# Moving batch 0's k and v tails from GpSimd's DMA queue to SyncE's, in halves of the heads

## Chip, cores and metric

The kernel runs on one core of one Trainium2 chip. The metric is the device time of one execution in microseconds, as the median of several runs; smaller is better. Times inside a run are counted from the first instruction of the profiled execution.

## The reference

Eight batches of eight heads, 576 positions, head dimension 64. Queries and keys pass a ReLU and are multiplied by a cosine and by a sine of the position, which doubles their width to 128; attention is linear (no softmax); a feed-forward layer with a leaky ReLU follows.

```python
theta = np.pi / 2.0 * pos / S                     # S = 576
phi(x) = concat([relu(x) * cos, relu(x) * sin])   # 64 -> 128
kv  = einsum('bhsf,bhsd->bhfd', phi(k), v)
z   = sum(phi(k), axis=2)
num = einsum('bhsf,bhfd->bhsd', phi(q), kv)
den = einsum('bhsf,bhf->bhs', phi(q), z) + 1e-6
x   = (num / den) -> (B*S, H*D) = (4608, 512)
out = leaky_relu(x @ w_in) @ w_out                # 512 -> 2048 -> 512, slope 0.01
```

## The kernel before

**Tiles.** The 576 positions of a batch are split into a main part of 512 (four positions on each of 128 partitions, `J = 4`) and a tail of 64. The main part of q, k or v of one batch is a tile of 128 partitions by 8 heads by 4 by 64; `load_main` (line 88) fetches it in halves of four heads for batch 0, in pieces of 1024 bytes. The tails of k and v are packed with two heads on the 128 partitions, even heads on even partitions and odd heads on odd ones: `load_kvtail` (line 98) makes one tile of 128 by 4 head pairs by 64 and fills it with two DMAs, one for each parity `o`, of 64 KB each in pieces of 256 bytes.

**Batch 0.** Its arrival starts the kernel and nothing can be computed ahead of it. SyncE issues, in this order (lines 147 to 155): q heads 0-3 and 4-7, k heads 0-3 (called k0 below), v heads 0-3 (v0), k heads 4-7 (k1), v heads 4-7 (v1), and then the eight pieces of the first weight matrix, `w1st`. GpSimd issues the four tail DMAs on its own queue (lines 210, 211) after it has made the constants.

**Compute of batch 0** (lines 554 to 608), written out by hand in the order in which each engine runs it:
- q is rotated (line 241 on VectorE, 239 on ScalarE), transposed on TensorE (line 366) and copied out of PSUM.
- `k_tail` rotates all four head pairs of k's tail with two VectorE instructions into `kpt`; `k_main(0, j, ...)` rotates heads 0-3 of the main part into `kpm`, five instructions on VectorE and three on ScalarE.
- `v_tail` multiplies v's tail by a parity mask, once for each parity (`vtail`: ScalarE line 222, VectorE line 224); `v_main` casts v's main part to fp16 into `vmain` (VectorE line 249, ScalarE line 247).
- `kv_half(0, 0, "t", 14)` runs 28 matmuls on a blank tile (line 168; they only keep TensorE busy), then the k-by-v products of heads 0-3: 16 matmuls over the main part (line 290) and two over the tail (line 299). ScalarE copies the sum out as `kv` (line 323).
- The same follows for heads 4-7: `k_main(0, j, ..., 4, 8)`, and `v_main` for these heads on GpSimd (line 249); `num_half(0, jp, 0)` forms numerator and denominator of heads 0-3 (line 417) and divides on VectorE (`den` line 392, `rden` line 396, `xp` line 397); then `kv_half(0, 1, "t", 2)`, transposes of the quotients (line 434), `num_half(0, jp, 1)` for heads 4-7, and the first feed-forward matmuls (line 460).

TensorE runs its program in the order in which it is written, so that `kv_half(0, 1)`, the transposes of `xp` and the two `num_half(0, jp, 1)` wait for one another in that order. After batch 0 the matmuls of the feed-forward layer follow without a break; batches 1 to 7 load their tails on SyncE's queue already.

**Queues.** A DMA on SyncE's queue signals one of eight semaphores, taken in turn. A DMA therefore is not issued before the one eight places ahead of it on that queue has landed. GpSimd's queue has semaphores of its own.

Of the kernel before, what the change touches and what calls it, by code (L numbers as in the profile page):

```python
# [9 lines left out]
dt = mybir.dt  # L10
# [3 lines left out]
P = 128  # L14
J = 4
# [3 lines left out]
def kernel(  # L19
# [14 lines left out]
    nc = tc.nc  # L34
    B, H, S, D = q.shape
# [43 lines left out]
    st = {}  # L79
# [8 lines left out]
    def load_main(nm, src, b, parts=(0, 1), soon=False):  # L88

        if parts[0] == 0:  # L90
            st[nm, b] = staged([P, H, J, D], f"{nm}st", soon)
        lo, hi = 4 * parts[0], 4 * parts[-1] + 4
        nc.sync.dma_start(  # L93
            st[nm, b][:, lo:hi],
            src[b, lo:hi, 0:MAIN, :].rearrange("h (p j) d -> p h j d", j=J),
        )

    def load_kvtail(nm, src, b, eng=nc.sync):

        t = kvtail.tile([P, H // 2, D], dt.float32, name=f"{nm}tl", tag="kvtail")  # L100
        v4 = src[b, :, MAIN:S, :].rearrange("(c o) p d -> o p c d", o=2)
        for o in range(2):
            eng.dma_start(t[o:P:2], v4[o])
        st[nm + "t", b] = t

    def load_qtail(i):
        if i == 0:
# [112 lines left out]
    def masked(eng, o, i, col):  # L220
        if eng is ACT:
            nc.scalar.activation(o, i, AF.Copy, scale=col)
        else:
            eng.tensor_scalar(out=o, in0=i, scalar1=col, scalar2=None, op0=ALU.mult)
# [37 lines left out]
        k_part(b, j, 0, eng_c, lo, hi)  # L262
        k_part(b, j, 1, eng_s, lo, hi)

    def k_tail(b, eng_c, eng_s):
        k_part(b, J, 0, eng_c)
        k_part(b, J, 1, eng_s)

    def k_part(b, j, part, eng, lo=0, hi=H):
        c = j if j < J else J + 1  # L270
        col, f = (cos_t, sin_t)[part][:, c : c + 1], part * D
        if j < J:
            o, i = st["kpm", b][:, lo:hi, j, f : f + D], st["k", b][:, lo:hi, j, :]
        else:
            o, i = st["kpt", b][:, :, f : f + D], st["kt", b]
# [5 lines left out]
    def v_tail(b, eng, both=(0, 1)):  # L281
        for o in both:
            masked(eng, vtail[:, :, o, 0:D], st["vt", b], odd[:, o : o + 1])

    def kv_mm(b, hg, ps):
        kpm, kpt = st["kpm", b], st["kpt", b]
# [31 lines left out]
    def kv_half(b, hg, where, blanks=0):  # L318
        ps = psum(where, [P, MAIN], dt.float32, "ps_kvh")
        idle(blanks, ps)  # L320
        ps = ps[:, 0 : 4 * NE]
        kv_mm(b, hg, ps)
        nc.scalar.copy(
            kv[b][:, 4 * hg : 4 * hg + 4, 0 : NE - 1],
            ps.rearrange("p (h e) -> p h e", h=4)[:, :, 0 : NE - 1],
        )
# [235 lines left out]
            idle(1, ps_idle)  # L562
    for j, eng in ((0, ACT), (1, DVE), (2, DVE), (3, ACT)):
        q_copy(0, j, eng)
    k_tail(0, DVE, DVE)
    for j, c, s in ((0, DVE, DVE), (3, ACT, ACT), (1, DVE, DVE), (2, DVE, ACT)):
        k_main(0, j, c, s, 0, 4)
    v_tail(0, ACT, (0,))
    v_tail(0, DVE, (1,))
    v_main(0, 0, 2, DVE)  # L570
    v_main(0, 2, 4, ACT)
    kv_half(0, 0, "t", 14)
    for j, c, s in ((0, DVE, DVE), (3, ACT, ACT), (1, DVE, DVE), (2, DVE, ACT)):
        k_main(0, j, c, s, 4, 8)
    v_main(0, 4, 6, POOL)
    v_main(0, 6, 8, POOL)
    num_half(0, 0, 0, "s", 2)
# [826 lines left out]
```

## Time and profile before

| | us |
|---|---|
| three runs | 270.31, 270.94, 272.93 |
| median | 270.94 |
| the profiled execution's own time | 271.15 |
| its span, first to last instruction | 269.2 |
| around the span (difference of the two) | 1.95 |

The page of the profile gives the busy time of each engine over the span, a strip of 40 slices, the DMA queues, the chain of work that ended last, and the costliest groups of instructions. TensorE (PE) is granted its full clock in every slice. Other views of the same trace are the timeline (start, duration, engine, source line, operation, output and input, count, and in square brackets how long the engine had been idle and what released it), the chain in order of time, the view of one tile or line (with "DMA to landing", the time from a DMA's issue to the arrival of its last byte), the waits, and the table by windows (busy us of each engine with its number of instructions, then TensorE's clock, the mean busy share of the 16 DMA engines, and the GB/s that they moved).

### The profile page before, as it was taken

The page shows a single profiled execution, that of the slowest core. Times are in us where ns is not written, and L with a number is a line of the kernel's source. Part 1 is how long each engine was busy: PE and PEld are TensorE (multiplying, and loading weights), DVE is VectorE, ACT ScalarE, POOL GpSimd, SP SyncE. Part 2 cuts the span into 40 slices and gives each one's busy share as a digit, 9 for nine tenths or more (in the row PEclk, how much of TensorE's full clock was granted, in tenths as well). Part 3 has the DMA queues.
Part 4 walks back from the last instruction along what each step waited for, and adds up shares of the span by engine and source line. Part 5 has one row for each costly group of instructions (what it writes and reads, how often), then busy time and mean ns, then how long its engine had stood idle before and what let it go on. Part 6 is the DMA issues. An engine that isn't in the chain of part 4 may idle for free.

```text
span 269.2 us, 6819 instructions
## 1 busy us (share of the span) xinstructions
PE 263.1 (98%) x2742; PEld 230.1 (85%) x2742; DVE 215.8 (80%) x486; ACT 203.9 (76%) x347; POOL 13.1 (5%) x25
## 2 busy tenths in 40 slices
PE   8989999999999999999999999999999999999994
PEld 6976465666899989999999999999999999999983
DVE  5785798698997898897979797979789968966453
ACT  8756556695989998997798799888968757787621
POOL 5057001000000000000000000000000000000000
PEclk9999999999999999999999999999999999999999
DMA  6999999979999969999999799987267232200314
GB/s 221 380 394 413 394 367 376 366 140 285 285 248 285 193 206 245 360 168 256 270 238 140 247 280 185 173 243 162 65 102 178 45 74 67 111 2 0 156 41 117
DMA packets 86190, 57.05 MB, mean 212 GB/s; under 512 B 55632, under 2 KB 81232, under 8 KB 85648
## 3 DMA queue, kind: packets, MB, share of 16 engines
q1 hardware_dynamic: 85584, 55.98, 79.3%
q8 instruction: 21, 0.34, 0.5%
q10 hardware_dynamic: 448, 0.39, 0.4%
q0 software_dynamic: 128, 0.26, 0.3%
q14 instruction: 9, 0.07, 0.1%
HBM read 36.70 MB, written 9.44 MB: 171 GB/s over the span
## 4 chain that ended last, share of the span: by engine, by line
PE 89%; DMA 5%; DVE 2%; SPq 1%; issue 1%; POOL 0%; ACT 0%; DVEq 0%
PE ps_h L782 31%; PE ps_o L883 30%; PE ps_h L460 5%; PE ps_o L476 5%; PE ps_h L496 5%; DMA vst<-in_v_dram 4%; PE ps_num L381 3%; PE ps_h L883 3%; PE ps_o L973 2%; PE ps_kv L290 2%; DMA xT<-xs 1%; SPq L93 1%; PE ps_qt L366 1%; PE ps_numh L417 1%; PE ps_kvh L290 1%; PE ps_kv L299 1%
## 5 line engine op out<-in xcount | busy, mean ns | idle before, releaser
L883 PEld LDWEIGHTS <-g 128*128 128x128 f16 x584 | 56.3, 98 | 5.3
L782 PE MATMUL ps_h<-xT,w 128*128 128x256 f16 x336 | 49.0, 273 | 0.0
L782 PEld LDWEIGHTS <-w 128*128 128x128 f16 x448 | 47.9, 113 | 1.1 <-issue 0.2
L252 DVE TENSOR_TENSOR u<-ps_h,u 128x512 f32<-128x512 f32 x56 | 38.3, 685 | 10.2 <-PE ps_h L782 10.0
L883 PE MATMUL ps_o<-w,g 128*128 128x256 f16 x288 | 41.4, 273 | 0.0
L782 PEld LDWEIGHTS <-wa 128*128 128x128 f16 x336 | 36.0, 113 | 1.0 <-issue 0.4
L795 ACT ACTIVATE g<-ps_h 128x512 f16<-128x512 f32 x56 | 33.9, 605 | 3.7 <-PE ps_h L782 3.5
L802 ACT COPY u<-ps_h 128x512 f32<-128x512 f32 x56 | 32.7, 584 | 4.9 <-PE ps_h L782 4.8
L809 ACT ACTIVATE g<-u 128x1024 f16<-128x1024 f32 x28 | 29.7, 1062 | 8.4 <-DVE u L252 8.2
L782 PE MATMUL ps_h<-xw,wa 128*128 128x256 f16 x224 | 33.6, 273 | 0.0
L883 PE MATMUL ps_o<-wb,g 128*128 128x256 f16 x232 | 32.2, 273 | 0.0
L883 PEld LDWEIGHTS <-gs 128*128 128x128 f16 x256 | 24.9, 98 | 2.4
L901 ACT COPY ob<-ps_o 128x512 f32<-128x512 f32 (+1 forms) x32 | 18.1, 564 | 9.4 <-PE ps_o L883 9.1
L397 DVE TENSOR_TENSOR xs<-ps_num,rden 128x512 f16<-128x512 f32 x28 | 19.4, 691 | 1.0
L883 PE MATMUL ps_o<-w,gs 128*128 128x256 f16 x120 | 17.5, 273 | 0.0
L792 ACT COPY ps_h<-ps_h 128x512 f32<-128x512 f32 x28 | 16.0, 573 | 1.6 <-PE ps_h L782 0.7
L255 DVE TENSOR_TENSOR gs<-g 128x1024 f16<-128x1024 f16 x16 | 11.0, 685 | 7.8 <-ACT g L809 7.6
L782 PE MATMUL ps_h<-xT,wa 128*128 128x256 f16 x112 | 16.8, 273 | 0.2 <-DVE u L252 0.2
L883 PE MATMUL ps_o<-wb,gs 128*128 128x256 f16 x120 | 16.9, 273 | 0.0
L782 PE MATMUL ps_h<-xw,w 128*128 128x256 f16 x112 | 16.8, 273 | 0.0
L252 DVE TENSOR_TENSOR ob<-ps_o,ob 128x512 f32<-128x512 f32 (+1 forms) x22 | 14.7, 670 | 1.3 <-ACT ob L901 0.9
L496 PE MATMUL ps_h<-xT,w 128*128 128x512 f16 (+1 forms) x72 | 15.1, 355 | 0.0
(128 smaller groups left out, 435.6 us busy)
## 6 DMA issues: line engine op xcount, KB each, us to landing
qst<-in_q_dram SPq DMA_DIRECT2D x7, 1024.0 KB, 6.6
out_dram<-ob SPq DMA_DIRECT2D x14, 512.0 KB, 2.9
kst<-in_k_dram SPq DMA_DIRECT2D x6, 1024.0 KB, 7.9
vst<-in_v_dram SPq DMA_DIRECT2D x6, 1024.0 KB, 7.0
w1st<-in_moe_w_in_dram SPq DMA_DIRECT2D x8, 512.0 KB, 10.0
w2st<-in_moe_w_out_dram SPq DMA_DIRECT2D x4, 1024.0 KB, 12.3
kst<-in_k_dram SPq DMA_DIRECT2D x4, 512.0 KB, 8.4
vst<-in_v_dram SPq DMA_DIRECT2D x4, 512.0 KB, 8.9
```

Of the source, the lines that this page charges most:

```text
L252: nc.vector.tensor_tensor(out=o, in0=a, in1=b, op=ALU.add)
L397: nc.vector.tensor_tensor(out=xs, in0=ps[:, :, 0 : 4 * NE].rearrange("p a (b e) -> p a b e", e=NE)[:, :, :, 0:D], in1=rden.rearrange("p (a ...
L460: nc.tensor.matmul(ps[:, m % 2, lo:hi], lhsT=w1[m // 4][c // 2][:, c % 2, m % 4 : 512 : 4], rhs=xT[:, c, lo:hi], start=(c == 0 and lo == 0 ...
L476: nc.tensor.matmul(ps, lhsT=st["g", g][:, m, tt * P : (tt + 1) * P], rhs=w2[:, m, :], start=(m == 0), stop=(m == NFT - 1),)
L496: nc.tensor.matmul(ps[:, lo:hi], lhsT=w1[m // 4][c // 2][:, c % 2, m % 4 : 512 : 4], rhs=st["xT", g][:, c, lo:hi], start=(c == 0 and lo == 0),
L782: nc.tensor.matmul(bank[:, p], lhsT=w(c), rhs=st["xb", g][n][:, c], start=(fresh and p == 0 and c == 0), stop=(c == 1), skip_group_check=True,
L792: nc.scalar.copy(bank1[bj], bank1[bi])
L795: nc.scalar.activation(st["g" + nm, g][:, 2 * t : 2 * t + 2], bank1[bi], AF.Lrelu)
L802: nc.scalar.copy(st["u", g, t][:, n], bank1[bi])
L809: nc.scalar.activation(st["gt", g][:, :, 1, 2 * t : 2 * t + 2], st["u", g, t], AF.Lrelu)
L883: nc.tensor.matmul(bank[..., lo:hi], lhsT=st[G2[n], g][:, m, pair * P : (pair + 1) * P], rhs=W2[n](m)[:, lo:hi], start=(fresh and m == 0), ...
L901: nc.scalar.copy(o_at(g, half_, col, pair), bank_of(bi, pair, pair is None))
```

## The change

The four tail DMAs of batch 0 leave GpSimd's queue. SyncE now issues eight, of 32 KB each: after k0 and v0 the tails of heads 0-3 (k even, k odd, v even, v odd), after k1 and v1 those of heads 4-7. The rotation and the masking of the tails are split in the same way: each half, two head pairs wide, is done after the main parts of its half, and not ahead of them. The tails of the other batches are untouched.

```diff
+    def load_kvtail(nm, src, b, lo=0, hi=H // 2):
+        if lo == 0:
+            st[nm + "t", b] = kvtail.tile(
+                [P, H // 2, D], dt.float32, name=f"{nm}tl", tag="kvtail"
+            )
         v4 = src[b, :, MAIN:S, :].rearrange("(c o) p d -> o p c d", o=2)
         for o in range(2):
-            eng.dma_start(t[o:P:2], v4[o])
-        st[nm + "t", b] = t
+            nc.sync.dma_start(st[nm + "t", b][o:P:2, lo:hi], v4[o, :, lo:hi])
...
-    load_main("k", k, 0, (0,))
-    load_main("v", v, 0, (0,))
-    load_main("k", k, 0, (1,))
-    load_main("v", v, 0, (1,))
+    for n in range(2):
+        load_main("k", k, 0, (n,))
+        load_main("v", v, 0, (n,))
+        load_kvtail("k", k, 0, 2 * n, 2 * n + 2)
+        load_kvtail("v", v, 0, 2 * n, 2 * n + 2)
...
-    load_kvtail("k", k, 0, nc.gpsimd)
-    load_kvtail("v", v, 0, nc.gpsimd)
...
+            c = slice(lo // 2, hi // 2)
+            o, i = st["kpt", b][:, c, f : f + D], st["kt", b][:, c]
...
+            masked(
+                eng, vtail[:, lo:hi, o, 0:D], st["vt", b][:, lo:hi], odd[:, o : o + 1]
+            )
...
-    k_tail(0, DVE, DVE)
     for j, c, s in ((0, DVE, DVE), (3, ACT, ACT), (1, DVE, DVE), (2, DVE, ACT)):
         k_main(0, j, c, s, 0, 4)
-    v_tail(0, ACT, (0,))
-    v_tail(0, DVE, (1,))
     v_main(0, 0, 2, DVE)
     v_main(0, 2, 4, ACT)
+    k_tail(0, DVE, DVE, 0, 4)
+    v_tail(0, ACT, (0,), 0, 2)
+    v_tail(0, DVE, (1,), 0, 2)
     kv_half(0, 0, "t", 14)
     for j, c, s in ((0, DVE, DVE), (3, ACT, ACT), (1, DVE, DVE), (2, DVE, ACT)):
         k_main(0, j, c, s, 4, 8)
+    k_tail(0, DVE, DVE, 4, 8)
+    v_tail(0, ACT, (0,), 2, 4)
+    v_tail(0, DVE, (1,), 2, 4)
     v_main(0, 4, 6, POOL)
```

What stands in a row after the change is shown at two places. In such rows the number after L is the source line; the changed kernel's lines stand one to seven higher. The first place is the start of SyncE's queue, where `kst` and `vst` are the main parts of k and v, `ktl` and `vtl` the tails, and DMAHW0 to DMAHW7 the eight semaphores of the queue. Before:

```order
L93 DMA kst<-in_k_dram 128x4x256
L93 DMA vst<-in_v_dram 128x4x256
L93 DMA kst<-in_k_dram 128x4x256
L93 DMA vst<-in_v_dram 128x4x256
L140 DMA w1st<-in_moe_w_in_dram 128x2x512 x2
L140 DMA w1st<-in_moe_w_in_dram 128x2x512 [waits DMAHW0_49]
```

After the change:

```order
L93 DMA vst<-in_v_dram 128x4x256
L106 DMA ktl<-in_k_dram 64x2x64 x2
L106 DMA vtl<-in_v_dram 64x2x64 x2
L93 DMA kst<-in_k_dram 128x4x256 [waits DMAHW0_49]
L93 DMA vst<-in_v_dram 128x4x256 [waits DMAHW1_49]
L106 DMA ktl<-in_k_dram 64x2x64 [waits DMAHW2_49]
L106 DMA ktl<-in_k_dram 64x2x64 [waits DMAHW3_49]
L106 DMA vtl<-in_v_dram 64x2x64 [waits DMAHW4_49]
L106 DMA vtl<-in_v_dram 64x2x64 [waits DMAHW5_49]
L142 DMA w1st<-in_moe_w_in_dram 128x2x512 [waits DMAHW6_49]
```

The four tails of a half stand behind its main parts; the second half of k and v now waits for the landing of q's halves, its k tails for k0 and v0, its v tails for the k tails of heads 0-3, and the weights for the v tails of heads 0-3.

The second place is VectorE's work for heads 4-7 of batch 0, up to the division of heads 0-3. Before:

```order
L241 TENSOR_SCALAR kpm<-kst,sin_t 128x4x64
L241 TENSOR_SCALAR kpm<-kst,cos_t 128x4x64
L392 TENSOR_SCALAR den<-ps_numh 128x8
L396 RECIPROCAL rden<-den 128x8
L397 TENSOR_TENSOR xp<-ps_numh,rden 128x2x256
```

After the change:

```order
L242 TENSOR_SCALAR kpm<-kst,sin_t 128x4x64
L242 TENSOR_SCALAR kpm<-kst,cos_t 128x4x64
L242 TENSOR_SCALAR kpt<-ktl,cos_t 128x2x64
L242 TENSOR_SCALAR kpt<-ktl,sin_t 128x2x64
L225 TENSOR_SCALAR vtail<-vtl,odd 128x2x64
L396 TENSOR_SCALAR den<-ps_numh 128x8
L400 RECIPROCAL rden<-den 128x8
L401 TENSOR_TENSOR xp<-ps_numh,rden 128x2x256
```

Three instructions that wait for the tails of heads 4-7 stand ahead of the division of heads 0-3, which needs none of them. Where heads 0-3 are prepared, the tail's instructions (four at full width before, on two engines) have become four of half width behind `vmain`; on ScalarE a masking of half width stands ahead of each of the two copies of `kv`.

More of the change, by code (lines that the diff above doesn't have):

```diff
@@ L263, in k_main, with k_tail @@
         k_part(b, j, 1, eng_s, lo, hi)
-    def k_tail(b, eng_c, eng_s):
-        k_part(b, J, 0, eng_c)
-        k_part(b, J, 1, eng_s)
+    def k_tail(b, eng_c, eng_s, lo=0, hi=H):
+        k_part(b, J, 0, eng_c, lo, hi)
+        k_part(b, J, 1, eng_s, lo, hi)
     def k_part(b, j, part, eng, lo=0, hi=H):
-        c = j if j < J else J + 1
-        col, f = (cos_t, sin_t)[part][:, c : c + 1], part * D
+        n = j if j < J else J + 1
+        col, f = (cos_t, sin_t)[part][:, n : n + 1], part * D
         if j < J:
```

6 lines of the change are left out of this document (1 added, 5 removed).

## The prediction

> **What bounds the kernel now.** I read the page first, then the chain of waits over the first 60 us, then the timeline of the first 20 us, the landing of single DMAs and the table by windows. The page:
>
> ```profile
> span 269.2 us, 6819 instructions
> PE 263.1 (98%) x2742; PEld 230.1 (85%) x2742; DVE 215.8 (80%) x486; ACT 203.9 (76%) x347; POOL 13.1 (5%) x25
> PE 89%; DMA 5%; DVE 2%; SPq 1%; issue 1%; POOL 0%; ACT 0%; DVEq 0%
> ```
>
> TensorE is busy for 263.1 of 269.2 us. No change that leaves its work alone can gain more than the 6.1 us between, and the start is one of the few places that hold them. The chain there:
>
> ```profile
> 3.56 10.78 DMA vst<-in_v_dram
> 14.39 1.18 POOL vmain L249 x2
> 15.61 0.42 PE ps_kvh L290 x8
> 16.18 0.39 ACT kv L323
> 16.61 0.41 PE ps_numh L417 x8
> 17.50 1.01 PE ps_h L460 x8
> 19.84 12.11 PE ps_h L460 x64
> ```
>
> v1 lands at 3.56 + 10.78 = 14.34; GpSimd casts it, TensorE closes k-by-v of heads 4-7, ScalarE copies it out at 16.18, the numerators start at 16.61, and from the first feed-forward matmuls at 17.5 on TensorE hardly stops. What the change gains or costs is therefore how far that 16.61 moves, unless a later wait takes it back.
>
> **Why v1 lands at 14.34.** Issue times, two landings, and the bytes moved:
>
> ```profile
> 1.80 0.51 SPq L93 DMA_DIRECT2D kst<-in_k_dram  x1
> 1.81 1.39 POOL L103 DMA_DIRECT2D ktl<-in_k_dram  x2
> 3.56 1.78 SPq L93 DMA_DIRECT2D vst<-in_v_dram  x1
> ```
>
> ```profile
> L93 SPq DMA_DIRECT2D qst<-in_q_dram x1: 492/492/492, 1.3 to 1.3; - x1
> DMA to landing us min/median/max: 4.6/4.6/4.6
> ```
>
> ```profile
> L93 SPq DMA_DIRECT2D kst<-in_k_dram x1: 507/507/507, 1.8 to 1.8; - x1
> DMA to landing us min/median/max: 8.5/8.5/8.5
> ```
>
> ```profile
> 2.00:5.84 3.84, 3.84 (x20) 2.74 (x19) 1.99 (x11) 3.45 (x9) 2.42 (x4) 1.00 0.94 314
> 5.84:10.27 4.43, 4.43 (x53) 3.92 (x52) 3.36 (x10) 3.15 (x6) 0.00 (x0) 1.00 1.02 355
> 10.27:14.34 4.07, 4.04 (x61) 3.56 (x59) 3.34 (x13) 3.45 (x10) 0.00 (x0) 1.00 1.07 398
> ```
>
> The second half of q lands at 1.26 + 4.57 = 5.84, k0 at 1.80 + 8.47 = 10.27. Up to 10.27 the DMA engines moved 3.84 x 314 + 4.43 x 355 = 2.78 MB (in KB: 1206 + 1573). q, k0 and all four tails are 1049 + 524 + 262 KB = 1.84 MB. So 0.94 MB, nearly two main parts, was moved for later transfers before k0 was whole: some of the 16 engines ran ahead and at least one lagged, and a transfer is only there when its slowest share is. The lag arises in just the window in which GpSimd's transfers pass. Had the shares been even, k0 would have been whole after 1835 - 1206 = 629 KB at 355 GB/s, or 1.8 us: at 7.6.
>
> **The change, part by part.**
>
> *Bytes.* They stay the same, 262 KB in pieces of 256 bytes. On SyncE's queue, behind a main part, the later batches show their price:
>
> ```profile
> L93 SPq DMA_DIRECT2D vst<-in_v_dram x1: 603/603/603, 108.1 to 108.1; - x1
> DMA to landing us min/median/max: 6.6/6.6/6.6
> ```
>
> ```profile
> L103 SPq DMA_DIRECT2D vtl<-in_v_dram x2: 620/1111/1602, 108.7 to 110.3; - x2
> DMA to landing us min/median/max: 4.7/5.4/6.2
> ```
>
> The main part lands at 114.65, the two 64 KB tails at 108.70 + 6.16 = 114.86 and 110.35 + 4.72 = 115.07. That is 0.21 us for 64 KB, so 0.42 us for the four 32 KB DMAs of a half (which this trace does not have: bounds 0.42, and 0.84 if each costs as much as a 64 KB one; I take 0.42, the bytes being what the rows share).
>
> *Landings, if the lag goes.* q as before, 5.84. A main part of 524 KB takes 524/398 = 1.3 us, the rate of the third window: k0 at 7.15. v0 8.5, tails of heads 0-3 8.9, k1 10.2, v1 11.5, tails of heads 4-7 12.0.
>
> *Landings, if it stays.* k0 is no longer mixed with 262 KB of tails, 0.66 us at 398: 9.6. v0 10.95, tails 11.35, k1 12.7, v1 14.0, tails 14.45.
>
> *SyncE's queue.* It issues eight DMAs that it did not issue before:
>
> ```profile
> L103 SPq DMA_DIRECT2D ktl<-in_k_dram x14: 609/744/2725, 27.0 to 157.5; - x14
> SPq L140 <- DMA vst<-in_v_dram: 0.5, 1, 0.5
> ```
>
> At 0.61 to 0.74 us each, 4.9 to 5.9 us of SyncE. The four of heads 0-3 run from 2.91 to 5.4-5.9; k1 and v1, issued at 2.91 and 3.56 before, follow at about 5.5 and 6.1 (they wait for q's landings at 4.51 and 5.84), still ahead of their turn on the engines. Then come the semaphore waits, whose like exists already (second row: 0.5 us). Without the lag the k tails of heads 4-7 go at 7.15 and 8.5 (k0, v0), the v tails at 9.1-9.3 and 9.7-10.0; w1st follows from about 10.4, behind v1 and the tails. Its first user is GpSimd, which is done with v at 14.39 + 1.18 = 15.57 now. q's second half needed 4.57 us from a queue nearly empty; so the weights land by 15.0 and are not late. With the lag they are issued from about 13.3 and land by 17.9 at worst, 0.4 us behind their first matmul at 17.5; that goes into the first rival's price.
>
> *Engines, heads 0-3.* Rows of the timeline:
>
> ```profile
> 9.26 3.22 PE L168 MATMUL ps_kvh<-blank 128*128 128x256 f16 x28
> 9.88 0.34 DVE L241 TENSOR_SCALAR kpt<-ktl,sin_t 128x256 f16<-128x256 f32 x1
> 10.30 0.35 DVE L241 TENSOR_SCALAR kpm<-kst,cos_t 128x256 f16<-128x256 f32 x1
> 11.57 0.50 ACT L222 ACTIVATE vtail<-vtl,odd 128x256 f16<-128x256 f32 x1
> 11.97 0.60 ACT L247 CAST vmain<-vst 128x512 f16<-128x512 f32 x1
> 12.35 0.69 PE L290 MATMUL ps_kvh<-vmain,kpm 128*128 128x65 f16 x16
> ```
>
> VectorE would start kpm at 9.62 instead of 10.30, but the 28 blank matmuls end at 12.48 and hold k-by-v at 12.35 whatever lands. Gain here: nothing. That cover is what a late landing would spend first.
>
> *Engines, heads 4-7.*
>
> ```profile
> 13.63 0.67 PE L417 MATMUL ps_numh<-kv,qpT 128*128 128x65 f16 x16
> 13.88 0.89 ACT L239 ACTIVATE kpm<-kst,sin_t 128x256 f16<-128x256 f32 x2
> 14.06 0.35 DVE L241 TENSOR_SCALAR kpm<-kst,cos_t 128x256 f16<-128x256 f32 x1
> 14.32 0.16 DVE L392 TENSOR_SCALAR den<-ps_numh 128x8 f32<-128x8 f32 x1
> 14.75 0.69 DVE L397 TENSOR_TENSOR xp<-ps_numh,rden 128x512 f16<-128x512 f32 x1
> 15.05 0.97 PE L290 MATMUL ps_kvh<-vmain,kpm 128*128 128x65 f16 x16 [0.32 <-POOL vmain L249]
> ```
>
> ```profile
> L241 DVE TENSOR_SCALAR kpm<-kst,sin_t x33: 342/476/481, 10.6 to 172.9; 128x512 f16<-128x512 f32 x21, 128x256 f16<-128x256 f32 x12
> ```
>
> On VectorE 256 columns take 0.342 and 512 take 0.476 us; by that slope 128 take about 0.28, and follow each other in some 0.2 (256 columns: 0.26). Six halves for three wholes: +0.4 us. ScalarE's two masks for one: about 0.44 each against 0.50, +0.35. With the lag gone, VectorE is through heads 0-3 at about 11.9, kpm of heads 4-7 at 13.2, the tails at 13.85: before 14.32, so that the division begins as soon as its matmuls are done, near 14.0. GpSimd has cast v by 12.8. ScalarE, whose kpm is behind its copy of kv, ends at 14.77 as before and then masks until 15.1: this is what ends last now. TensorE runs the 16 matmuls from 14.77 and the tail from 15.3, ScalarE copies from 15.5, the numerators start at 15.95 instead of 16.61. **Sum: -0.6 us**; between -0.4 (a half mask on ScalarE as dear as a whole one) and -0.9 (as if it cost nothing).
>
> The same page of the notes has two rules that weigh here, and they disagree. The Trainium skill, "DMA: Bandwidth & Descriptors", section "Latency and other measured facts", says that two of the DMA engines are usually slower, with contention on the ports of the GpSimd queue's descriptor rings as its best guess. By it the lag would go, and the sum would be the -0.6 above; the trace agrees in that one lag arises while that queue is in use. The section "Issuing engines are not separate DMA queues" of the same page says that all issuers share the same 16 engines and that the choice of issuer saves only issue time. By it the lag would stay, which is the first rival.
>
> **Rivals.**
>
> *The lag stays: slower.* Then the tails of heads 4-7 land at 14.45, behind v1, and three VectorE instructions that wait for them stand ahead of the first division. 14.45 + 0.7 = 15.15 for `den` instead of 14.32; both quotients come 0.8 later, the second at 17.35 instead of 16.55, and TensorE waits for its transpose. The earlier v1 (0.3) hides a part. Price: **+0.4 us** (0.2 to 0.8, the upper end with 0.84 us for four tails). It decides from a landing at 13.6 on: 13.6 + 0.7 is the old 14.32. For it: a lag once there stays on the queue (from k0 at 10.27 to v1 at 14.34 three main parts took 1.36 each, none caught up). Against it: where SyncE alone fed the engines, at 108 us, tails came in straight order behind the main part.
>
> *The gain is given back.* TensorE starts 0.6 earlier and waits 0.6 later, on VectorE:
>
> ```profile
> 36.00:40.00 4.00, 4.00 (x38) 2.52 (x36) 4.00 (x13) 3.11 (x4) 0.00 (x0) 1.00 0.98 370
> ```
>
> VectorE is full there, though TensorE does not wait (4.00 of 4.00). Against it: VectorE's loads come earlier too. Price: 0.
>
> *Starvation: slower by more.* The eight semaphores hold bytes back: four small DMAs take places that held 512 KB each, the engines run dry between v1 and the weights, and each dry spell of about 1 us shifts all loads to 40 us. Prefetched weights and TensorE's work cover some 1.5 us. Price +1 to +3 us. Against it: the issue times above.
>
> **How the numbers follow.** The sum is made against the profiled execution, 271.15 (span 269.2 and 1.95 around it): 270.55. It lies 0.21 above the median of 270.94, from which I count: 270.94 - 0.6 = **270.3**. Chances: forecast 0.55 (own range 269.8 to 270.7); lag stays, 271.3, 0.25; given back, 270.9, 0.13; starvation, 272 to 274, 0.07. The range takes in the first three and the spread of the runs: 269.3 to 272.0. One per cent is 2.7 us, about what a measurement of this kernel can tell from no change; the bound of 0.9 on the gain lies far inside, and only starvation reaches it on the other side. Faster 0.03, same 0.92, slower 0.05.
>
> **What would show it.** Right: k0 lands near 7, v1 near 11.5, tails of heads 4-7 before 13.6; the copy of kv of heads 4-7 starts near 15.5 and waits for ScalarE's mask, not for GpSimd; L460 starts 0.6 earlier. Wrong: v1 still lands at or after 14; `den` waits for the tails; gaps in the DMA share between 11 and 15 us; weights that land after 16; or an earlier L460 with an unchanged end.

## The result: 0.7% slower

| | before | after |
|---|---|---|
| median of 20 runs each, us | 271.35 | 273.21 |
| lowest and highest, us | 270.21, 273.40 | 271.52, 276.54 |
| the profiled execution's own time, us | 271.15 | 272.53 |
| ratio to before, with its 95% interval | | 1.0070 (1.0052 to 1.0089) |

The change costs about 1.9 us. That is under one per cent, so "about the same" came true, but 273.2 lies above the range (269.3 to 272.0), and the sign of the forecast was wrong. With 20 executions the median of the kernel before is 271.35, 0.4 above the 270.94 from which the forecast was counted. The highest time after the change (276.54) and the profiled execution of e6 below (273.57) were slow ones (over 1.5% above the fastest of the same kernel), which the ratios leave out.

The page of the changed kernel:

```profile
span 270.8 us, 6827 instructions
PE 263.2 (97%) x2742; PEld 229.4 (85%) x2742; DVE 216.2 (80%) x489; ACT 204.5 (76%) x348; POOL 10.2 (4%) x21
PE 77%; DMA 12%; DVE 7%; SPq 2%; issue 1%; DVEq 0%
```

TensorE works as long as before (263.2 against 263.1 us), so the whole difference is idle time. In the chain of work that ended last, DMA's share has gone from 5% to 12%. Pieces of that chain over the first 45 us, in order of time, tell what kind of wait it is:

```profile
2.34 7.44 DMA vst<-in_v_dram
...
9.80 0.61 SPq L106
...
13.65 7.28 DMA w1st<-in_moe_w_in_dram
...
21.00 14.52 DMA qst<-in_q_dram
...
35.54 2.98 DVE qp L242 x8
```

Before, the chain went through v1 and was on TensorE from 17.5 us on. Now it runs from v0's landing at 9.78 through SyncE, which issues three tails (line 106) one after another and then, from 11.75, weights (line 142), through a weight piece, and through q of batch 1, which VectorE awaits until 35.5. Of that path nothing is arithmetic until 35.54.

SyncE's issues, first of the kernel before (one row for all eight weight pieces), then of the changed one:

```profile
5.38 9.65 SPq L140 DMA_DIRECT2D w1st<-in_moe_w_in_dram  x8
```

```profile
5.76 0.59 SPq L93 DMA_DIRECT2D kst<-in_k_dram  x1
6.40 1.12 SPq L93 DMA_DIRECT2D vst<-in_v_dram  x1
8.38 2.02 SPq L106 DMA_DIRECT2D ktl<-in_k_dram  x2
10.45 1.26 SPq L106 DMA_DIRECT2D vtl<-in_v_dram  x2
11.75 2.37 SPq L142 DMA_DIRECT2D w1st<-in_moe_w_in_dram  x3
```

The first weight piece goes out at 11.75 instead of 5.38. Most of that is issuing, at 0.6 to 0.7 us for each of the eight tails; SyncE waited for landings twice, 0.8 us for k0 and 0.8 us for v0. What the DMA engines did meanwhile is in the last two numbers of each row of the table by windows (the share of the time that they were busy, and GB/s), before (two windows) and after:

```profile
12.00:14.00 2.00, 1.97 (x39) 1.69 (x37) 1.29 (x5) 1.38 (x5) 0.00 (x0) 1.00 1.07 406
16.00:18.00 2.00, 1.76 (x32) 1.50 (x30) 1.42 (x4) 1.45 (x3) 1.81 (x4) 1.00 1.04 392
```

```profile
10.00:12.00 2.00, 2.00 (x30) 1.83 (x28) 1.58 (x8) 1.77 (x5) 0.00 (x0) 1.00 0.95 319
12.00:14.00 2.00, 1.97 (x37) 1.61 (x33) 1.06 (x5) 1.57 (x4) 0.98 (x2) 1.00 0.68 163
14.00:16.00 2.00, 0.92 (x17) 0.67 (x16) 1.53 (x6) 0.80 (x3) 0.19 (x1) 1.00 0.90 275
16.00:18.00 2.00, 1.37 (x27) 1.25 (x28) 1.79 (x7) 0.87 (x2) 1.18 (x2) 1.00 0.90 229
18.00:20.00 2.00, 2.00 (x23) 1.84 (x21) 1.23 (x4) 0.89 (x2) 0.78 (x2) 1.00 0.98 337
```

From 10 to 20 us the engines move 2 x (319 + 163 + 275 + 229 + 337) = 2646 KB; before, in the same windows, it was 2 x (389 + 406 + 393 + 392 + 392) = 3944. The 1298 KB that are missing are 3.3 us of loading, and they are not made up: q of batch 1 lands at 21.00 + 14.52 = 35.5, before at 32.6 (issued at 18.45, 14.13 to landing), 2.9 later.

Only part of what is missing is engines that stand idle. Before, a busy share of 1.04 went with 392 GB/s; at that rate the shares after the change (0.95, 0.68, 0.90, 0.90, 0.98) would have moved 3323 KB, an estimate. So about 620 KB were lost to idle engines, from 12 to 14 us above all, and about 680 to engines that were busy and moved less. The 256-byte pieces of the tails pass up to about 14 us and can account for some of it, but not for 0.90 and 229 GB/s from 16 to 18. What makes the engines slow there is not settled.

Two more places of the start, in the timeline:

```profile
8.54 3.22 PE L171 MATMUL ps_kvh<-blank 128*128 128x256 f16 x28
14.40 0.29 DVE L242 TENSOR_SCALAR kpt<-ktl,cos_t 128x128 f16<-128x128 f32 x1 [1.35 <-DMA ktl<-in_k_dram]
14.76 0.40 ACT L223 ACTIVATE vtail<-vtl,odd 128x128 f16<-128x128 f32 x1 [0.74 <-DMA vtl<-in_v_dram]
14.99 0.17 DVE L396 TENSOR_SCALAR den<-ps_numh 128x8 f32<-128x8 f32 x1
15.53 0.38 ACT L327 CAST kv<-ps_kvh 128x260 f16<-128x260 f32 x1 [0.37 <-PE ps_kvh L303]
16.41 1.18 POOL L250 CAST w<-w1st 128x512 f16<-128x512 f32 x2 [2.22 <-DMA w1st<-in_moe_w_in_dram]
23.05 2.13 PE L464 MATMUL ps_h<-xT,w 128*128 128x512 f16 x9 [0.34 <-DVE w L250]
```

The copy of kv of heads 4-7 is early, as forecast (15.53; forecast 15.5; before 16.18). But `den` waits behind the tails' rotation (14.99 instead of 14.32), GpSimd then stands 2.22 us for the first weights, and TensorE has to wait for weights at 23.05.

Where TensorE fell behind is told by two of its rows, the first feed-forward matmuls and the transposes of batch 1's q, before and after:

```profile
17.34 1.18 PE L460 MATMUL ps_h<-xT,w 128*128 128x256 f16 x8
35.23 0.61 PE L366 MATMUL ps_qt<-ident,qp 128*128 128x128 f16 x8
```

```profile
17.77 1.18 PE L464 MATMUL ps_h<-xT,w 128*128 128x256 f16 x8
36.48 0.62 PE L370 MATMUL ps_qt<-ident,qp 128*128 128x128 f16 x8
```

It is 0.43 us late at the first and 1.25 at the second, and ahead of the second it does not stand idle: in this execution that time had gone before, in waits for the quotients and for weights. The late q would have cost about as much by itself. In e8 (below) the transposes start 0.96 us after q's landing; so the kernel before, with q there at 32.6 and the transposes at 35.23, could have borne a delay of 1.7 us (an estimate), and the delay is 2.9. Late weights and late q come of the same late loads, and TensorE pays them side by side, not one after the other.

### The profile page after: what moved, and what is told of

Same layout as the page of the kernel before. It is cut to its first block, busy times and chain, and to the rows that moved or that the text cites. A ratio compares the mean times of both kernels' runs of the same rounds, so it can differ in the third digit from the quotient of the medians.

```text
span 270.8 us, 6827 instructions
## 1 busy us (share of the span) xinstructions
PE 263.2 (97%) x2742; PEld 229.4 (85%) x2742; DVE 216.2 (80%) x489; ACT 204.5 (76%) x348; POOL 10.2 (4%) x21
## 4 chain that ended last, share of the span: by engine, by line
PE 77%; DMA 12%; DVE 7%; SPq 2%; issue 1%; DVEq 0%
PE ps_h L789 30%; PE ps_o L890 30%; DMA qst<-in_q_dram 5%; PE ps_h L500 4%; PE ps_num L385 3%; PE ps_h L890 3%; DMA vst<-in_v_dram 3%; DMA w1st<-in_moe_w_in_dram 3%; PE ps_o L980 2%; PE ps_kv L294 2%; DMA xT<-xs 1%; DVE kpm L242 1%; DVE qp L242 1%; DVE wb L256 1%; DVE xp L401 1%
## 5 line engine op out<-in xcount | busy, mean ns | idle before, releaser
L890 PE MATMUL ps_o<-w,gs 128*128 128x256 f16 x120 | 17.5, 273 | 0.0
```

What stands on the lines that cost most here:

```text
L890: nc.tensor.matmul(bank[..., lo:hi], lhsT=st[G2[n], g][:, m, pair * P : (pair + 1) * P], rhs=W2[n](m)[:, lo:hi], start=(fresh and m == 0), ...
```

## The experiments

The theory that came out of the two traces, called Q in the expectations: **SyncE's turn**. A DMA of any size takes one of eight places in SyncE's queue, costs SyncE about 0.6 us to issue, and cannot be issued before the one eight places ahead has landed. Of the eight places ahead of the first weights six hold tails, almost without bytes, so when SyncE gets to the weights the DMA engines are nearly done, and the bytes of a new transfer start to move only 1 to 2 us after its issue (below, e3 and e9). The main rival, V: the division waits for the tails and everything behind it is late. A second, P: the pieces of 256 bytes on SyncE's queue are what costs. Ratios are to the kernel before, run on the same chip; the other columns are from one profiled execution each.

| run | small transfers on SyncE's queue | first w1st issued | second w1st landed | q of batch 1 landed | ratio (95%) |
|---|---|---|---|---|---|
| the change | 8, ahead of w1st | 11.75 | 19.17 | 35.5 | 1.0070 (1.0052, 1.0089) |
| e14, the change again | 8 | 11.36 | 17.62 | 34.9 | 1.0059 (1.0034, 1.0084) |
| e3, eight of 1 KB | 8 | 12.62 | 20.37 | 36.5 | 1.0075 (1.0044, 1.0105) |
| e6, four of 1 KB | 4 | 9.08 | 17.22 | 33.5 | 1.0003 (0.9967, 1.0039) |
| e8, eight of 1 KB, late | 8, behind w1st | 4.69 | 17.17 | 35.9 | 1.0087 (1.0051, 1.0123) |
| e5, division first | 8 | 11.09 | 20.11 | 35.6 | 1.0065 (1.0032, 1.0098) |
| e13, heads 4-7 by GpSimd | 4 | 9.17 | 17.66 | 33.2 | 1.0021 (0.9991, 1.0050) |
| e1, four whole tails | 4 | 8.29 | 16.21 | 32.6 | 1.0023 (0.9994, 1.0053) |
| e7, e11, those with whole compute | 4 | 8.02, 8.36 | 16.37, 17.56 | 31.9, 34.1 | 0.9992 (0.9960, 1.0024), 1.0006 (0.9975, 1.0037) |
| e2, halves, GpSimd's queue | 0 | 4.81 | 17.18 | 32.7 | 1.0035 (1.0012, 1.0058) |
| before | 0 | 5.38 | 17.02 | 32.6 | 1 |

The landing of the second w1st does not sort the runs (17.62 in e14 with a loss, 17.66 in e13 without one that can be told); that of q of batch 1 does: 34.7 us or later in every run with eight (e4, e9 and e10 below too), 34.1 or earlier in the others, of which only e12, whose engines start late for another reason, shows a loss of that size.

**e3: the turn with no bytes.** The kernel before, with eight 1 KB transfers where the change has its tails; the copies are read by nobody and the rest of the kernel is untouched.

```diff
-    load_main("k", k, 0, (0,))
-    load_main("v", v, 0, (0,))
-    load_main("k", k, 0, (1,))
-    load_main("v", v, 0, (1,))
+    scrap = const.tile([16, 128], dt.float32, name="scrap")
+    for n in range(2):
+        load_main("k", k, 0, (n,))
+        load_main("v", v, 0, (n,))
+        for m in range(4 * n, 4 * n + 4):
+            nc.sync.dma_start(scrap[:, 16 * m : 16 * m + 16], q[0, m, 0:16, 0:16])
```

> The kernel before, with its tails on GpSimd's queue, plus eight DMAs of 1 KB on SyncE's queue at the eight places where the change puts the tails; nothing reads what they load. Turns and issue time without the tails' bytes, pieces or order of compute. Theory Q: the second half of v and the weights are issued as late as in the change (first weights near 11.5 to 13 us), the engines run dry at 13 to 17 us, and the time is +1.3 to +2.5 us against before. Theories V and P: the tails themselves are where they were, so within 0.4 us of before.

Measured: 1.0075, the whole loss. SyncE's issues and the table by windows of this run:

```profile
9.47 3.10 SPq L154 DMA_DIRECT2D scrap<-in_q_dram  x4
12.62 2.80 SPq L140 DMA_DIRECT2D w1st<-in_moe_w_in_dram  x4
```

```profile
12.00:14.00 2.00, 1.27 (x24) 1.06 (x24) 1.95 (x8) 0.47 (x2) 0.00 (x0) 1.00 0.40 116
14.00:16.00 2.00, 1.96 (x42) 1.79 (x42) 1.49 (x7) 1.17 (x4) 1.17 (x2) 1.00 0.90 261
16.00:18.00 2.00, 1.61 (x27) 1.17 (x24) 1.76 (x5) 1.38 (x3) 1.17 (x2) 1.00 1.02 271
20.00:22.00 2.00, 0.65 (x4) 0.47 (x5) 0.00 (x0) 0.58 (x1) 1.17 (x2) 1.00 1.05 397
```

The first of the last four is issued at 9.47, as k0 lands at 9.46; the weights follow at 12.62, and TensorE, with the same matmuls, is busy 0.65 of 2 us at 20 to 22. Neither the tails' bytes nor the halves nor the place of the rotation is in this kernel, so that they are not needed for the loss, and P is refuted. The mix of the delay is another one, though: SyncE waits 2.7 us for k0 and 1.5 for v0, which land later beside GpSimd's transfers (9.46 and 11.30), where the change waited 0.8 and 0.8. From 16 to 18 us the engines are fully busy (1.02) at 271 GB/s: here too they are slow for longer than they are idle, and without 256-byte pieces on SyncE's queue.

The first w1st also tells how a new transfer starts when little else is queued; the two windows are of the same run:

```profile
L140 SPq DMA_DIRECT2D w1st<-in_moe_w_in_dram x1: 423/423/423, 12.6 to 12.6; - x1
DMA to landing us min/median/max: 3.9/3.9/3.9
```

```profile
13.40:13.60 0.20, 0.20 (x5) 0.18 (x3) 0.20 (x2) 0.07 (x1) 0.00 (x0) 1.00 0.06 21
13.60:13.80 0.20, 0.20 (x3) 0.14 (x2) 0.20 (x2) 0.20 (x2) 0.00 (x0) 1.00 0.47 78
```

Issued at 12.62, its bytes begin to move between 13.6 and 13.8, some 1.1 us later. From there 512 KB take until 16.52, 2.8 us, where 398 GB/s would need 524/398 = 1.3. So the smaller part of the 3.9 us is the wait for the first bytes.

**e6: half as many.** As e3, with the four of the first round only.

> The kernel before, with four transfers of 1 KB (read by nobody) on SyncE's queue behind the first main parts of k and v: half of the eight of the run that repeated the loss with no bytes (ratio 1.0075, first weights issued at 12.62, engines at 72 to 160 GB/s from 12 to 14 us). It tells whether the price goes with the number of transfers or with a threshold. Theory Q: with four turns instead of eight SyncE comes to the first weights by 8.5 to 10 us, while k1 and v1 are still being moved; no microsecond from 10 to 20 us falls below 350 GB/s, the weights land within 1 us of before, and the median is within 0.5 us of before (ratio 0.998 to 1.002). If each transfer has its own price: half the loss, +0.9 to 1.0 us (ratio 1.0035).

Measured: 1.0003, no loss to be seen; the first weights go out at 9.08, while k1 and v1 are still moving. The windows hold 389 and 394 from 10 to 14 us; one window, 14 to 16, falls to 308 at a busy share of 0.99, which Q did not have. So four cost nothing measurable where eight cost 2 us. Half of that price (1.0035) still lies inside the interval, so that this run does not tell a threshold from a price for each transfer; of the other runs with four, e7's interval leaves it out.

**e8: the same eight, later.** The eight 1 KB transfers behind the last w1st.

```diff
     for i in range(NB):
         for cp in range(2):
             load_w1(i, cp)
+    scrap = const.tile([16, 128], dt.float32, name="scrap")
+    for m in range(8):
+        nc.sync.dma_start(scrap[:, 16 * m : 16 * m + 16], q[0, m, 0:16, 0:16])
```

> The kernel before with the eight 1 KB transfers (read by nobody) on SyncE's queue behind the last of the first feed-forward weights, instead of behind v0 and v1: the same number of turns, when some 4 MB of transfers are already in flight. Theory Q: what costs is that the turn comes while few bytes are queued; here the first weights are issued at 5.4 us as before and land as before (15.7, 17.0, ...), the engines stay at 380 GB/s and more up to 26 us, and what is late is only the second weights, which have slack; the median is within 0.5 us of before (ratio 0.998 to 1.002). If eight extra turns cost whatever their place: +1.5 to 2 us (ratio 1.0055 to 1.0075).

Measured: 1.0087. The expectation of Q failed, and the rival in it, that eight turns cost whatever their place, came true. The weights land as before (second at 17.17), but the gap only comes later:

```profile
15.83 9.68 SPq L158 DMA_DIRECT2D scrap<-in_q_dram  x8
25.64 0.89 SPq L144 DMA_DIRECT2D w2st<-in_moe_w_out_dram  x2
```

```profile
24.00:26.00 2.00, 2.00 (x11) 1.02 (x9) 1.93 (x3) 1.02 (x1) 2.00 (x2) 1.00 0.04 9
```

```profile
36.83 0.62 PE L369 MATMUL ps_qt<-ident,qp 128*128 128x128 f16 x8 [1.48 <-DVE qp L244]
```

Each of the eight waits for one w1st to land (9.68 us for eight issues), and when the bytes of the last w1st have been moved nothing is queued: 9 GB/s from 24 to 26 us. TensorE does not notice then (2.00 of 2.00), but q of batch 1 lands at 26.63 + 9.23 = 35.9 instead of 32.6, and there it stands 1.48 us. Eight turns cost 2.0 and 2.4 us at the two places tried: both times q of batch 1 is late by more than the 1.7 us that could be borne.

**e5: the division no longer waits.** In the changed kernel, the tail instructions of heads 4-7 on VectorE and ScalarE go behind the first division.

```diff
-    k_tail(0, DVE, DVE, 4, 8)
-    v_tail(0, ACT, (0,), 2, 4)
-    v_tail(0, DVE, (1,), 2, 4)
     v_main(0, 4, 6, POOL)
     v_main(0, 6, 8, POOL)
     num_half(0, 0, 0, "s", 2)
+    k_tail(0, DVE, DVE, 4, 8)
+    v_tail(0, ACT, (0,), 2, 4)
+    v_tail(0, DVE, (1,), 2, 4)
```

> The changed kernel with one thing moved: VectorE's and ScalarE's tail instructions of heads 4-7 stand behind the first division instead of ahead of it, so the division no longer waits for those tails (in the changed kernel it starts at 14.99 us, before at 14.32). Queues and transfers stay as in the change. Theory Q (SyncE's turn: the eight small transfers make it wait for earlier landings, so the first weights are issued at 11.75 instead of 5.38 us): the weights are issued at 11.5 to 12 us and land as late as in the changed kernel (16.4, 19.2, 20.9), all later loads keep their 2.5 to 3 us, and the median stays 1.2 to 1.9 us above the kernel before (ratio 1.004 to 1.007), though the division starts near 13.5. Theory V (the division that waits for the tails costs the time): most comes back, within 0.5 us of before (ratio 1.000 to 1.002).

Measured: 1.0065, as the change. The 0.7 us that `den` had waited came back in the profile (the copy of the second quotient's transpose is at 17.0 instead of 17.7) and were spent a few us later, for weights:

```profile
20.84 0.30 PE L464 MATMUL ps_h<-xT,w 128*128 128x256 f16 x1 [1.31 <-POOL w L250]
```

V is refuted as what sets the end: the wait of `den` is real, but it hides in the wait for weights. An earlier attempt at the same question, **e4**, gave the rotation and one mask of heads 4-7 to GpSimd:

```diff
-    k_tail(0, DVE, DVE, 4, 8)
-    v_tail(0, ACT, (0,), 2, 4)
-    v_tail(0, DVE, (1,), 2, 4)
...
+    k_tail(0, POOL, POOL, 4, 8)
+    v_tail(0, ACT, (0,), 2, 4)
+    v_tail(0, POOL, (1,), 2, 4)
```

> The changed kernel with the rotation and one mask of the tails of heads 4-7 on GpSimd behind its cast of v, so that VectorE reaches the division of heads 0-3 without waiting for a tail. All queues as in the change. Theory V: the first den starts near 13.3 instead of 15.0 us, and most of the 1.9 us comes back (+0.3 us or less against before). Theory Q: den starts near 13.3 too, but the weights land as late as in the change (16.4, 19.2, 20.9), the matmuls wait for them, and the time stays at +1.2 to +1.9 us against before.

Measured: 1.0093 (1.0058 to 1.0129). `den` started at 13.22, but GpSimd takes 0.72, 0.71 and 0.61 us for instructions that take VectorE 0.28, and the copy of kv came at 17.37 instead of 15.53. The run put a new wait in the place of the old one and decides nothing.

**e13 and e14: the turn given back.** In the changed kernel, the tails of heads 4-7 alone return to GpSimd's queue, in halves as in the change; beside it, on the same chip, the changed kernel.

```diff
-        load_kvtail("k", k, 0, 2 * n, 2 * n + 2)
-        load_kvtail("v", v, 0, 2 * n, 2 * n + 2)
+        if n == 0:
+            load_kvtail("k", k, 0, 0, 2)
+            load_kvtail("v", v, 0, 0, 2)
...
+    load_kvtail("k", k, 0, 2, 4, nc.gpsimd)
+    load_kvtail("v", v, 0, 2, 4, nc.gpsimd)
```

> The changed kernel with the four tails of heads 4-7 on GpSimd's queue, issued behind GpSimd's setup as in the kernel before (in the run before this one they stood ahead of it and held up the identity matrix by 3.4 us). Theory Q: the DMA engines keep 350 GB/s and more from 10 to 20 us, the third w1st lands by 19 us (20.9 in the changed kernel), the first feed-forward matmuls come 0.5 us or more earlier than in the changed kernel, and the ratio to the kernel before is 1.000 to 1.004; beside it the changed kernel itself stays at 1.006 to 1.009. Rival (halves and eight transfers as such): both alike within 0.2%.

> The changed kernel once more, on the same chip as the run before and after this one. 1.006 to 1.009 by every theory; its first w1st is issued between 11 and 12.5 us and lands near 16.4, the second between 18.5 and 20.5.

Measured: 1.0021 and 1.0059, medians 271.55 and 272.57: 1.0 us came back with four of the eight turns, and what is left cannot be told from no change. The two intervals overlap a little, and half the price of eight would fit e13 as well. In e13's profile the third w1st landed at 19.05, and one window (14 to 16 us) stood at 318 GB/s, a little under what was expected; in e14's the window from 12 to 14 was at 98, and its second w1st landed at 17.62, ahead of the 18.5 to 20.5 expected. The two profiled executions alone would not have told them apart (spans 269.4 and 269.5): e13's first feed-forward matmul was not earlier, its k0 having landed at 9.15 against 7.99 in e14. The medians of 12 runs each carry the verdict. The first try at this, **e12**, had the four GpSimd issues ahead of GpSimd's setup.

> The changed kernel with one part undone: the four tails of heads 4-7 go by GpSimd's queue as before, those of heads 0-3 stay on SyncE's behind v0; halves of the rotation and masks, order on all engines as in the change. SyncE has four small transfers instead of eight. Theory Q in its present form (the first w1st is issued too late, since four turns of SyncE wait for k0, v0 and the first tails, and bytes move only some 2.4 us after the issue): the first w1st is issued by 8.5 us, no two microseconds from 10 to 20 fall under 330 GB/s, the third w1st lands by 19 us (20.9 in the changed kernel), and what is left is the price of the halves on VectorE and ScalarE that the second and the first run showed (1.0035 and 1.0023): ratio 1.001 to 1.004. Rival (the loss comes with the halves and the eight transfers as such, not with SyncE's turn): 1.006 to 1.009.

Measured: 1.0113 (1.0078 to 1.0148), although the DMA engines never fell under 384 GB/s from 10 to 22 us and the second w1st landed at 15.21. The waits show what went wrong: VectorE stood 3.4 us for the identity matrix that GpSimd makes, and the start was 1.8 to 2.9 us late.

That late start is an error of the experiment and says nothing on the change, but for one thing: a full queue does not help a kernel whose engines start late. (The 2.4 us to the first bytes that the expectation counts with are 1.1 by the rows of e3 and 2.0 by those of e9.)

**e1, e7 and e11: four whole tails.** SyncE brings the tails of all heads behind v0 as four transfers of 64 KB. e1 keeps the rotation and masks in halves; e7, and e11 once more, make them whole, behind the main parts of heads 0-3.

```diff
-        load_kvtail("k", k, 0, 2 * n, 2 * n + 2)
-        load_kvtail("v", v, 0, 2 * n, 2 * n + 2)
+        if n == 0:
+            load_kvtail("k", k, 0)
+            load_kvtail("v", v, 0)
```

> The changed kernel with the four tails of batch 0 left whole (64 KB each, all on SyncE's queue behind v of heads 0-3), computed by halves as in the change. Theory Q (the queue: eight small DMAs take eight of the turns on eight semaphores and 5 us of SyncE, so the weights are issued 6.4 us later and the DMA engines run dry from 12 to 18 us): with four turns fewer the first weights are issued near 8 us, their first piece lands before 15.5, no dry window, and the time is back at before or below it (-0.8 to +0.3 us against before). Theory V (VectorE's order: the division of heads 0-3 stands behind tails that land late): the tails land by 10.5, so it too expects before or below. Theory P (256-byte pieces on SyncE's queue are what costs): the same 1024 pieces are on the same queue, so +1.5 to +2 us as in the change.

> Four whole tails (64 KB each) on SyncE's queue behind v0, as in the first run, but rotated and masked whole as in the kernel before: 3 instructions on VectorE and one on ScalarE less than with halves. The first run, with halves, took 1.0023 (0.9994 to 1.0053) of the kernel before, though its own profile was 0.7 us shorter. Theory H (the halves of the rotation and masks cost 0.4 us on VectorE and 0.35 on ScalarE, and that is what the first run lost beside its gain of the earlier landings): the median comes to 0.2 to 0.7 us below the kernel before (ratio 0.9975 to 0.9995), v1 lands by 13.2. Theory N (the start does not set the median, loads in mid-kernel do, whose spread over runs is larger): ratio 0.999 to 1.004, no different from the first run.

> The four whole tails on SyncE's queue with the rotation and masks whole, once more (first time: ratio 0.9992, 0.996 to 1.0024, the profiled execution 1.8 us shorter than that of the kernel before). Theory H (the start is really shorter and the runs only spread): 0.996 to 0.999, and the profiled execution again has its first feed-forward matmul at least 0.6 us earlier than 17.34. Theory N (the first time's profile had quick blank matmuls, 5.2 us against 6.1, and nothing of the change shows in the median): 0.998 to 1.002.

Measured: 1.0023, 0.9992 and 1.0006. e1's 1.0023 is 0.6 us, above the 0.3 that Q allowed, though its interval reaches below that. With four turns the stream holds in e1 (385 to 401 GB/s from 10 to 22 us); in e11 one window (12 to 13 us) fell to 229, without a loss in the median. e7's profile looked like a gain, its span 267.4 us; e11 is the same code and had 271.0. Neither median differs from the kernel before; theory N (nothing of it shows in the median) holds. This is the best arrangement found with SyncE alone, and it is no better than the kernel before.

**e2: the halves alone.** The changed kernel's compute in halves, with four whole tails on GpSimd's queue as before.

```diff
-        load_kvtail("k", k, 0, 2 * n, 2 * n + 2)
-        load_kvtail("v", v, 0, 2 * n, 2 * n + 2)
...
+    load_kvtail("k", k, 0, eng=nc.gpsimd)
+    load_kvtail("v", v, 0, eng=nc.gpsimd)
```

> The compute of the change (tails rotated and masked by halves, behind the main parts) with the four whole tail DMAs back on GpSimd's queue. All of the queue part is undone. Theory Q: before's landings come back (v of heads 4-7 near 14.3, weights from 15.7), the time is within 0.4 us of before. Theory V: the tails are there by 10 us, so nothing stands in front of the division: within 0.4 us of before as well. A theory that the six half-width instructions (+0.4 us VectorE, +0.35 us ScalarE) are what costs: +1 us or more.

Measured: 1.0035 (1.0012 to 1.0058), some 0.9 us, with no late weights (second at 17.18). That is more than the 0.4 us that Q and V allowed and near the 1 us of the theory that the halves cost. Alone among the runs without a gap its interval leaves 1 out; e1 and e13, also in halves, stand at 1.0023 and 1.0021, e7 and e11 with whole compute at 1.000. That the halves cost a few tenths of a us is likely by these five together; its size stays open. e2 and e3 together would make 1.011 where the change has 1.0070: either the two costs hide one another or the intervals hold the difference, and how the 1.9 us are shared between them is not shown.

**e9 and e10: bytes ahead of the tails.** e5 with one w1st (e9) or two (e10) issued between v1 and the tails of heads 4-7.

```diff
         load_main("v", v, 0, (n,))
+        for m in range(1 * n):      # e10: 2 * n
+            load_w1(0, m)
...
-    for i in range(NB):
-        for cp in range(2):
-            load_w1(i, cp)
+    for m in range(1, 2 * NB):      # e10: 2, 2 * NB
+        load_w1(m // 2, m % 2)
```

> The run with the division first (ratio 1.0065, 0.9032 not exceeded: interval 1.0032 to 1.0098), with one transfer moved: the first w1st (512 KB) goes between v1 and the four tails of heads 4-7, so that SyncE's queue holds 512 KB more while it waits for its turns. The same number of small transfers, the same instructions on all engines. Theory Q (the engines run dry because the queue holds nothing but small transfers while SyncE waits): no microsecond between 12 and 18 us falls under 300 GB/s, the second w1st lands by 18 us instead of 20.1, the first feed-forward matmuls do not wait, and at least 1.2 us come back (ratio 1.000 to 1.002). If the eight transfers cost by their number alone: no change (1.005 to 1.008).

(The words "0.9032 not exceeded" in it are a slip of the pen and mean nothing.)

> As the run before it, with two w1st (1 MB) ahead of the four tails of heads 4-7. Theory Q: the engines stay at 370 GB/s and more up to 20 us; but the tails of heads 4-7 land another 1.3 us later, near 15.5 to 16, and k-by-v of heads 4-7 has to wait for them: its copy is at 16.5 to 17 instead of 16.18 in the kernel before, while the feed-forward block is not late. Ratio 1.000 to 1.004, no better than with one ahead. If the number of transfers sets the price: 1.005 to 1.008.

Measured: 1.0058 (1.0027 to 1.0089) and 1.0102 (1.0070 to 1.0133). Q's numbers failed in both; e9 came out as the rival in its expectation had it (a price by the number of small transfers alone), e10 above both. SyncE's issues and the windows of e9:

```profile
8.28 0.43 SPq L142 DMA_DIRECT2D w1st<-in_moe_w_in_dram  x1
9.63 1.26 SPq L106 DMA_DIRECT2D ktl<-in_k_dram  x2
12.24 2.92 SPq L142 DMA_DIRECT2D w1st<-in_moe_w_in_dram  x4
```

```profile
13.00:14.00 1.00, 1.00 (x22) 0.86 (x19) 0.61 (x3) 1.00 (x3) 1.00 (x2) 1.00 0.39 87
14.00:14.20 0.20, 0.16 (x5) 0.14 (x5) 0.20 (x1) 0.01 (x1) 0.07 (x1) 1.00 0.09 19
14.20:14.40 0.20, 0.20 (x11) 0.20 (x10) 0.20 (x1) 0.00 (x0) 0.19 (x1) 1.00 0.90 97
```

The gap is still there, because 512 KB are too few. The tails' turn begins when v0 lands (9.6), four issues take 2.6 us, and the bytes of the next w1st begin to move 2.0 us after that, at about 14.2. At 398 GB/s the queue would have to hold 4.6 x 398 = 1.8 MB at 9.6; it held k1, v1 and one w1st, 1.6 MB, part of it already moved. The profiled span was 1.4 us shorter than e5's (269.5, 270.9), but the median followed little. In e10 the gap is smaller (127 GB/s from 15 to 16 us), but the tails land at 16.6, and TensorE stands 2.3 us for them: the other side of the same trade. Small transfers on this queue come too late behind big ones, and starve the engines when nothing big is ahead.

## Why the prediction was wrong, point by point

- **The step that failed** is in the part on SyncE's queue: "so the weights land by 15.0 and are not late". It held the landing against the first user, GpSimd's cast at 15.57. It should have held it against the stream. By the prediction's own numbers the tails of heads 4-7 were to land at 12.0 and the weights, issued at 10.4, at 15.0: one weight piece, 1.3 us of loading at 398 GB/s, in 3.0 us, so that 1.7 us of loading were lost. What the runs showed in its place: the first piece, issued at 11.75, landed at 16.36 (4.6 us after its issue, as forecast; it is the issue that came late), the second at 19.17 instead of 17.02, 3.3 us of loading were missing by 20 us, and q of batch 1 was 2.9 late. And the trace of before showed that the casting engine had no slack, in rows of the same timeline:

```profile
15.72 1.17 POOL L249 CAST w<-w1st 128x512 f16<-128x512 f32 x2 [0.16 <-DMA w1st<-in_moe_w_in_dram]
17.07 1.17 POOL L249 CAST w<-w1st 128x512 f16<-128x512 f32 x2 [0.19 <-DMA w1st<-in_moe_w_in_dram]
```

  Both casts of weights already waited for their landing, and VectorE waited 1.4 us for q of batch 1; TensorE itself could bear 1.7 us there. A gap moves every load up to 35 us.
- **The rival was right and its chance wrong.** Starvation was named with its mechanism, its place ("between v1 and the weights") and its price (+1 to +3 us, 272 to 274). It got 0.07 "against it: the issue times above", and these times were the evidence for it. Its 1.5 us of cover is near the 1.7 that the traces give: 2.9 - 1.7 = 1.2, and TensorE was 1.25 late at that place in the profiled execution. The rest of the 1.9 us between the medians is not accounted for. Its mechanism is right in part: "the engines run dry" holds for about half of the missing bytes, the others are engines that were busy and slow, which the prediction did not name.
- **SyncE's issue times** were nearly right for k1 and v1 (5.5 and 6.1; 5.76 and 6.40) and 1.3 us early for the rest (weights 10.4; 11.75), since k0 and v0 landed 1.2 and 1.3 later than forecast, and each turn waits for such a landing.
- **The lag** of the slowest share neither went nor stayed. k0 landed at 8.37 (forecast 7.15 without the lag, 9.6 with it); SyncE alone gave 7.5 to 8.7 in eight other profiles, GpSimd's queue beside it 8.6 to 9.5 in five (e2, e3, e6, e8, e13), 10.27 in the one that the forecast was built on, and 7.68 in e12, where GpSimd's transfers, half as large, were issued 0.6 us earlier. Between the middles of the two groups, 7.9 and 9.1, lie 1.2 us, of which the bytes mixed in explain up to 262/398 = 0.7; so that queue goes with some 0.5 us of lag, e12 apart, but 10.27 was the worst of its kind, and the term of -0.6 was counted from it. By the Trainium skill, "DMA: Bandwidth & Descriptors", section "Latency and other measured facts", two of the DMA engines are usually slower, with contention at the descriptor rings of GpSimd's queue as a best guess. The traces bear that out in part: the last of k0's 16 shares came 1.8 to 3.4 us behind the first with GpSimd's four transfers beside it (0.7 in e12), and still 0.8 to 2.0 with SyncE's queue alone. By the Trainium skill, the section "Issuing engines are not separate DMA queues" of the same page, starting DMAs on several engines saves only the sequencer's time, usually small beside the DMA itself. Here giving that saving up put the first weights off by 6.4 us, places in the queue included, and cost 0.7%.
- **Blank matmuls.** "Gain here: nothing" for heads 0-3 was wrong: the 28 blank matmuls started at 8.54 instead of 9.26 and let the first copy of kv run 0.77 earlier (12.43). They did so in e2 as well (8.67), with GpSimd's queue. Part of every profile's earlier start is that the profile of before had a late one.
- **Heads 4-7.** The tails landed at 14.7 instead of 12.0, so that rival 1's place was reached too: `den` at 14.99 (rival: 15.15, forecast: about 14.0). By e5 it does not add to the end. The costs of the halves were sized well: 0.28 on VectorE, 0.40 on ScalarE (forecast 0.28 and 0.44). That the copy of kv came at 15.53, as forecast, is luck: ScalarE was done with `kpm` at 14.01, not at 14.77, and then stood 0.74 us for v's tail, which landed 2.7 us later than forecast; the two errors cancel. And the numerators behind it started at 16.41, not at 15.95, since the transposes of the late quotients stand ahead of them on TensorE.

## To carry to other kernels

A transfer in a queue that issues by turns costs a place, whatever its size: count the bytes that stay queued while the issuer waits, and compare them with the issue time plus the latency to the first byte (in e9 1.8 MB, 4.6 us at full rate), before you count what the moved bytes cost. When loads bound a stage, hold a later landing against the stream and not against its first user: ask for how long afterwards every consumer already waits for its load. And a landing that a forecast is counted from should be seen in more than one execution.

## Not expected of the hardware

Two profiles of the same code (e7, e11) differ by 3.6 us of span, 1.9 us of it between 82 and 89 us, where a load of k (batch 4) was late: ScalarE's wait for it is 0.3 us in e7 and 2.1 in e11. The same wait took 2.6 us in e2. What delays that load in some executions was not settled. Scatter of this kind makes the intervals here some 0.4 to 0.7% wide, and a gain of the size forecast (0.6 us, 0.2%) could hardly have been shown by runs of 12.

That DMA engines can be busy and yet move two thirds of the usual bytes (e3 from 16 to 18 us, e6 and e13 from 14 to 16 at shares of 0.99 and 0.96 and 308 and 318 GB/s) was not expected either. In e6 and e13 it came without an idle stretch ahead of it. Its cause is open.
